# Attention with interleaved MLP work: which max product of a half cycle without filling goes to the filling's PSUM bank

## The chip, the cores and the metric

The kernel runs on one core of a Trainium2 chip. The metric is the device time of one execution in microseconds (us), lower is better. The engines are PE (TensorE: matmul, with its weight loads, PEld, beside it), DVE (VectorE), ACT (ScalarE), POOL (GpSimd) and SP (SyncE, which issues transfers here). PE writes its products to PSUM, which has eight banks of 128 x 512 float32 numbers; DVE and ACT read them there. A bank can take a new product only when the last reader of the old one is done, so a product often waits for a reader.

## The reference

One transformer block with adaptive layer norm, in float32, on 2048 rows of width 512. Attention has 32 query heads of width 16 and a single shared key and value head; the MLP has 1376 hidden units.

```python
def _A_ref(x, wq, wk, wv, wo):              # 32 heads, Dh = 16, one key and value head
    q = (x @ wq).reshape(B, S, H, Dh).transpose(0, 2, 1, 3)
    k = x @ wk
    v = x @ wv
    scores = jnp.einsum("bhqd,bkd->bhqk", q, k) * (Dh ** -0.5)
    p = softmax(scores, axis=-1)
    o = jnp.einsum("bhqk,bkd->bhqd", p, v)
    return o.transpose(0, 2, 1, 3).reshape(B, S, H * Dh) @ wo

def _B_ref(x, w1, b1, w2, b2):
    return gelu(x @ w1 + b1) @ w2 + b2

sa, ca, ga, sb, cb, gb = silu(c) @ w_mod    # six rows of 512
x = x + ga * _A_ref(layernorm(x) * (1 + ca) + sa, wq, wk, wv, wo)
x = x + gb * _B_ref(layernorm(x) * (1 + cb) + sb, w1, b1, w2, b2)
```

## The kernel before

The queries are cut into 8 blocks of 256 rows, and each block into 8 units of 4 heads: 64 units. The softmax takes each row's true maximum, so all scores are computed twice, once for the maximum and once for the exponential:

- **Max products** (`m`, line 509): a 128 x 512 piece of scores, rows of queries against 512 keys. A DVE reduction (`mx`, line 514) takes the maximum of each row. The maxima go through a transpose and POOL into rows of the query tile `qst`, so that the second score product subtracts them by itself. Max products run several units ahead of their exponentials.
- **Score products** (`e`, line 589): keys against queries. ACT takes the exponential (`p`, line 590).
- **Value products** (`acc`, line 601): eight for each pair of key tiles, from `p` and the values.

Both kinds of score product use 64 of PE's 128 rows; side 0 and side 1 (the last number of an `m` or `e` name) run beside each other.

All engines run in the order in which the Python code records the instructions. A loop over units and pairs of key tiles writes one **cycle** per turn, as two **half cycles**. Each half cycle holds four `e` products, as a rule four `m` products and, after them, the eight `acc` products of the pair before (each two weight loads and products in the trace). In the trace a half cycle can be taken from its first `e` product to that of the next one.

Between these the kernel records **filling**: the rest of the work of a block whose attention is done (output projection `wops`, second layer norm and its transposes `tp`, the MLP's products `w1ps` and `w2ps`), and query projections `qps` early on. A job hands its products over in batches of about six (or four transposes); a batch is spread over the two half cycles of a cycle, half of the rows in each. Where no job has a batch ready, which a job says by asking for some turns of delay, both half cycles are written by the function `plain`. `clock` counts turns, four to a cycle. `queue` lists the jobs, each with the turn at which it goes on and a mark for a delay of two turns or more ("planned"); `holder` holds a job that must not be interrupted.

PSUM's banks are given out by tags: three banks for `m` in rotation, three for `e` (`e0` to `e2`) in an order that `plain` passes in `banks`, one (`v`) for `acc`, and one, `x`, for the filling. In `plain`, `maxes(s, n)` makes a list of n max products of side s, and `issue` merges the two lists. In a half cycle with two max products on each side the order of PE's queue is: e, e, m (side s, the first of `ms`), m (side t, the first), e, m (side t, the last), m (side s, the last), e. Sides are s = 1 and t = 0. Line 1332 may send the last max product of side t, the third of the four, to bank x. It does so where no job is held and where no planned job is due within two turns (`soon`).

Of the kernel before, what the change touches and what calls it, by code (L numbers as in the profile page):

```python
# [48 lines left out]
def adaln_mqa_mlp(  # L49
# [16 lines left out]
    _, S, D = x.shape  # L66
# [71 lines left out]
    clock = [0]  # L138
# [10 lines left out]
    def due():  # L149
        now = [p for p in pending if p[0] <= clock[0]]  # L150
        pending[:] = [p for p in pending if p[0] > clock[0]]
        for _, fn in now:
            fn()
# [26 lines left out]
    def half(one, s):  # L180

        ps, a, b_, first_, last_ = one
        rows = slice(64 * s, 64 * s + 64)
        nc.tensor.matmul(ps, a[rows], b_[rows], start=first_ and s == 0, stop=last_ and s == 1)  # L184
# [391 lines left out]
    def sexp(u, K, j, s, bank):  # L576

        w = blocks[units[u][0]][1]
        qst = qsts[u]
        assert u in placed  # L580
        if (u, K) not in ptiles:
            ptiles[u, K] = att.tile([P, 2, 2, 512], F32, name=f"p{u}_{K}", tag="p", bufs=3)
        e = psum.tile([P, 512], F32, name=f"e{u}_{K}_{j}_{s}", tag="x" if bank == "x" else f"e{bank}", bufs=1)
        rows = slice(64 * s, 64 * s + 64)
        if w == 512:
            kt, rhs = K, qst[rows, j, :]
        else:
            kt, rhs = 2 * K + j, qst[rows].rearrange("p j n -> p (j n)")
        nc.tensor.matmul(e, ks[rows, kt * P:(kt + 1) * P], rhs, start=True, stop=True)  # L589
        nc.scalar.activation(ptiles[u, K][:, j, s, :], e, AF.Exp, scale=0.25)  # L590
# [488 lines left out]
    def prep_w2():  # L1079
        rp = wts_pool["rest"]  # L1080
        wfs = {}

        def load(f):
            fw = min(P, F - f * P)
            wf = wfs[f] = rp.tile([P, D], F32, name=f"w2f{f}", tag="wf", bufs=3)
            if fw < P:
                nc.gpsimd.memset(wf, 0.0)
            nc.sync.dma_start(out=wf[:fw], in_=w2[f * P:f * P + fw, :])

        def work(f):  # L1090
            nc.gpsimd.tensor_tensor(out=wfs[f], in0=wfs[f], in1=gb, op=ALU.mult)
            split(w2H[:, f, :], w2L[:, f, :], wfs[f], nc.gpsimd, nc.gpsimd)

        return prepare(NF, load, work)
# [3 lines left out]
    queue = []  # L1098
    holder = []
# [14 lines left out]
    def resume():  # L1114

        go_on(holder[0])

    def advance():

        for job in holder or list(queue):  # L1120
            while not held and job[0] <= clock[0] and go_on(job):
                pass
            if held or holder:
                break
# [4 lines left out]
    def take():  # L1129
        advance()  # L1130
        return held.pop() if held else None
# [3 lines left out]
    mp = Max()  # L1135
# [129 lines left out]
    def products(batch):  # L1265

        return sum(b_.shape[-1] * (4 if b_.dtype == F32 else 1) for _, _, b_, _, _ in batch) / 512
# [7 lines left out]
    def issue(*groups):  # L1275

        at = [0.0] * len(groups)
        groups = [list(g) for g in groups]
        while any(groups):
            g = min((g for g in range(len(groups)) if groups[g]), key=lambda g: at[g])  # L1280
            length, fn = groups[g].pop(0)
            fn()
            at[g] += length

    def mixture(a, b):

        out = []
        while a or b:
            if a:
                out.append(a.pop(0))  # L1290
            if b:
                out.append(b.pop(0))
        return out

    def end_step(u, K):

        pv(u, K)
        if K == steps[u] - 1:
            finish_unit(u)
            if units[u][1] == NQ - 1:  # L1300
                put_off(rest(units[u][0], units[u][0] == len(blocks) - 1))

    behind = None
    for u in range(NU):
        for K in range(0, steps[u], 2):
            goal = lead[u] + (lead[u + 1] - lead[u]) * (K + 2) / steps[u]
            goal = min(goal, first[u + QBUFS] if u + QBUFS < NU else first[NU])
            n = max(0, 2 * round((goal - mp.done) / 2))

            def maxes(s, n, first_=1.0, held=None):  # L1310
                return [(1.0 if i else first_, lambda i=i: mp.step(s, held if i == 2 else None)) if mp.has(s) else (0.0, lambda: None)
                        for i in range(n)]

            def exps(s, which):
                return [(1.0, lambda K=K, j=j, bank=bank: sexp(u, K, j, s, bank)) for K, j, bank in which]

            def halves(batch, s):

                total = products(batch)
                ahead = AHEAD if total > BATCH - 0.5 else (BATCH - (1.5 if batch[-1][4] else 0.5)) / total  # L1320
                return [(ahead * products([one]), lambda one=one: half(one, s)) for one in batch]

            def plain(s, K, t, n, banks):

                a, b_, c_, d = banks
                one = mixture(exps(s, [(K, 0, a), (K, 1, c_)]), maxes(s, n))
                other = maxes(t, n)

                soon = any(planned and time <= clock[0] + 2 for time, _, planned in queue)
                if not holder and not soon and mp.has(t) and n > 1:  # L1330
                    other[-1] = 1.0, lambda: mp.step(t, tag="x", bufs=1)
                issue(one, exps(t, [(K, 0, b_)]) + other + exps(t, [(K, 1, d)]))

            X, Y = K, K + 1

            due()
            batch = take() if behind else None
            if batch:  # L1340
                groups = [mixture(maxes(1, n // 2, 0.0), exps(1, [(X, 0, 0), (X, 1, 1), (Y, 0, 2)])),
                          halves(batch, 0) + exps(0, [(X, 0, 0)])]
                issue(*(reversed(groups) if batch[0][3] else groups))
            else:
                plain(1, X, 0, (n + 2) // 4, (1, 2, 0, 1))
            clock[0] += 1
            due()
            if behind:
                end_step(*behind)
            clock[0] += 1  # L1350
            due()
            if batch:

                reduces = [] if batch[-1][4] else None

                def go_on_():
                    resume()
                    for fn in reduces or ():
                        fn()

                issue(mixture(maxes(0, n // 2, 0.0, reduces), exps(0, [(X, 1, 0), (Y, 0, 1), (Y, 1, 2)])),
                      halves(batch, 1) + [(0.0, go_on_)] + exps(1, [(Y, 1, 0)]))
                advance()
            else:
                plain(1, Y, 0, n // 4, (2, 0, 1, 2))
            clock[0] += 1
            due()
            end_step(u, X)
            behind = (u, Y)
            clock[0] += 1  # L1370
            if state["mods"] and state["q"] == 0 and w2H is None:
                w2H = att.tile([P, NF, D], F32R, name="w2H", tag="bigH")
                w2L = att.tile([P, NF, D], F32R, name="w2L", tag="bigL")
                preps["w2"] = prep_w2()
            if clock[0] >= prepared[0] + PREP and weights and weights[0] in preps:
                prepared[0] = clock[0]
                if next(preps[weights[0]], 0) == 0:
                    weights.pop(0)
# [51 lines left out]
```

## Time and profile before

| what | value |
|---|---|
| time, median of 3 runs | 1599.63 us (1597.88 to 1600.57) |
| the profiled execution's own time | 1599.49 us |
| span of the profiled execution | 1597.6 us |
| busy: PE, DVE, ACT, POOL | 1560.3, 1412.9, 1203.0, 666.1 us |
| granted TensorE clock, mean | 0.996 |
| max products, and their reductions on DVE | 2048 each, 682 ns a reduction |
| exponentials on ACT | 2048, 599 ns each |
| first half cycles without filling in a block, ahead of `tp` | at 324.48 and 327.78 us (block 0) |
| those ahead of `w1ps` | at 342.11 and 345.06 us (block 0) |

A row of the page's list of groups reads: line, engine, operation, tile written <- tiles read, shapes, count | busy us, mean ns of one | idle time of the engine just before these instructions, and what ended it. A row of the timeline reads: start in us, length in us, engine, line, operation, tiles, how many are merged in the row, and in brackets the idle time ahead of it with what ended that. PE's ends are modelled. A row of a windows answer reads: stretch in us, its length, then for PE, PEld, DVE, ACT and POOL the busy time with the number of instructions, then the granted clock and the transfers.

### The profile page before, as it was taken

To read this page: it belongs to the slowest core of one execution; us is meant where nothing else is said; L and a number is where in the kernel's file an instruction comes from. 1 tells how busy PE (TensorE), PEld (TensorE's weight loads), DVE (VectorE), ACT (ScalarE), POOL (GpSimd) and SP (SyncE) were. 2 spreads that over 40 slices of the span, in tenths; PEclk is the share of its full clock that TensorE was granted. 3 is DMA by queue.
4 is the path that set the end of the run, shared out by engine and by line. 5 is a ranking of instruction groups with operands and counts; after the bars stand their busy time and mean duration, and the time that the engine had idled before them with its cause. 6 is when DMAs were issued, how large, how long until landed. Compare 5 with 4: busy or idle time off the path is not lost.

```text
span 1597.6 us, 41064 instructions
## 1 busy us (share of the span) xinstructions
PE 1560.3 (98%) x16369; PEld 1006.3 (63%) x16369; DVE 1412.9 (88%) x2473; ACT 1203.0 (75%) x2393; POOL 666.1 (42%) x1176
## 2 busy tenths in 40 slices
PE   5999999999999999999999999999999999999998
PEld 3466665557665676657665676656666576656667
DVE  6899999899999998999989999999999999999715
ACT  5577778778777887778877887778877787778853
POOL 4445344747422571246413462234602474225711
PEclk8999999999999999999999999999999999999999
DMA  7136312313022220303112120213112130122232
GB/s 257 73 109 205 117 68 71 125 32 107 17 63 65 68 68 25 103 17 106 32 44 84 53 85 22 78 42 98 42 35 91 42 98 18 62 72 64 80 132 74
DMA packets 79285, 121.59 MB, mean 76 GB/s; under 512 B 15774, under 2 KB 52382, under 8 KB 78836
## 3 DMA queue, kind: packets, MB, share of 16 engines
q1 hardware_dynamic: 79076, 118.95, 23.2%
q8 instruction: 128, 2.10, 0.6%
q14 instruction: 65, 0.53, 0.1%
q10 hardware_dynamic: 16, 0.00, 0.0%
HBM read 91.13 MB, written 27.27 MB: 74 GB/s over the span
## 4 chain that ended last, share of the span: by engine, by line
PE 90%; DVE 6%; DMA 2%; POOL 1%; SPq 1%; ACT 0%; issue 0%; DVEq 0%; POOLq 0%
PE acc L601 30%; PE m L509 22%; PE e L589 17%; PE w1ps L184 8%; DVE mx L514 5%; PE w2ps L184 4%; PE wops L184 2%; PE qps L184 1%; PE w2ps L178 1%; DMA xt<-in_A_x_dram 1%; PE w1ps L178 1%; PE tp L184 1%; PE kps L160 1%; DMA qst<-dq 1%; DVE st L807 0%; DMA os<-drs 0%
## 5 line engine op out<-in xcount | busy, mean ns | idle before, releaser
L514 DVE TENSOR_REDUCE mx<-m 128x1 f32<-128x512 f32 x2048 | 1271.4, 682 | 107.6 <-PE m L509 81.3
L590 ACT ACTIVATE p<-e 128x512 f32<-128x512 f32 x2048 | 1069.4, 599 | 311.1 <-PE e L589 233.2
L509 PE MATMUL m<-ks,qst 64*128 64x512 f32 x2048 | 823.9, 425 | 17.4 <-DVE mx L514 11.0
L589 PE MATMUL e<-qst,ks 64*128 64x512 f32 x2048 | 739.1, 409 | 2.8 <-ACT p L590 1.5
L601 PE MATMUL acc<-p,va 128*32 128x256 f32 x8192 | 550.5, 386 | 0.6 <-DMA qst<-dq 0.6
L509 PEld LDWEIGHTS m<-ks,qst 64*128 64x128 f32 x2048 | 364.1, 184 | 185.8 <-DVE mx L514 157.0
L589 PEld LDWEIGHTS e<-qst,ks 64*128 64x128 f32 x2048 | 366.6, 185 | 85.2 <-ACT p L590 59.5
L601 PEld LDWEIGHTS acc<-p,va 128*32 128x32 f32 x8192 | 214.9, 109 | 220.6 <-issue 115.7
L184 PE MATMUL w1ps<-h2H,w1t 64*128 64x256 f32 x1232 | 236.3, 288 | 0.0
L558 POOL TENSOR_SCALAR mt<-turned 8x32 f32<-8x32 f32 x256 | 53.2, 208 | 362.4 <-DVE turned L564 350.4
L184 PEld LDWEIGHTS w1ps<-h2H,w1t 64*128 64x128 f32 x1232 | 184.2, 185 | 31.7 <-issue 23.0
L184 PE MATMUL w1ps<-h2L,w1t 64*128 64x256 f32 x616 | 169.4, 275 | 0.0
L184 PE MATMUL w2ps<-w2H,gH 64*128 64x512 f32 x286 | 118.1, 413 | 0.0
L184 PE MATMUL w2ps<-w2L,gH 64*128 64x512 f32 x286 | 117.4, 411 | 0.0
L184 PE MATMUL w2ps<-w2H,gL 64*128 64x512 f32 x286 | 117.4, 410 | 0.0
L184 PEld LDWEIGHTS w1ps<-h2L,w1t 64*128 64x128 f32 x616 | 113.8, 185 | 0.0
L920 POOL TENSOR_SCALAR tt<-tt 128x256 f32<-128x256 f32 x77 | 31.1, 404 | 162.8 <-ACT tt L919 162.8
L744 POOL TENSOR_TENSOR os<-os 128x256 f32<-128x256 f32 x28 | 20.6, 734 | 100.9 <-DMA os<-drs 100.2
L921 POOL TENSOR_TENSOR tt<-tt,z 128x256 f32<-128x256 f32 x77 | 57.1, 741 | 6.4
L135 POOL TENSOR_TENSOR gL<-z,gH 128x256 fp32r<-128x256 f32 x77 | 56.8, 738 | 6.4
L931 POOL TENSOR_TENSOR z<-tt,z 128x256 f32<-128x256 f32 x77 | 56.5, 733 | 6.0
L930 POOL TENSOR_TENSOR tt<-tt,z 128x256 f32<-128x256 f32 x77 | 56.7, 736 | 0.0
(188 smaller groups left out, 1498.2 us busy)
## 6 DMA issues: line engine op xcount, KB each, us to landing
w1t<-dw SPq DMA_DIRECT2D x82, 512.0 KB
qst<-dq SPq DMA_DIRECT2D x128, 64.0 KB
do<-oc SPq DMA_DIRECT2D x64, 128.0 KB
dw<-w1s SPq DMA_DIRECT2D x11, 512.0 KB
xt<-in_A_x_dram SPq DMA_DIRECT2D x4, 1024.0 KB
dq<-qH SPq DMA_DIRECT2D x16, 256.0 KB
dq<-qL SPq DMA_DIRECT2D x16, 256.0 KB
qst<-dq SPq DMA_DIRECT2D x128, 32.0 KB
```

The lines of the kernel that those rows point to most:

```text
L135: eng_l.tensor_tensor(out=dst_l, in0=src, in1=raw(dst_h), op=ALU.subtract)
L178: nc.tensor.matmul(ps, a, b_, start=first_, stop=last_)
L184: nc.tensor.matmul(ps, a[rows], b_[rows], start=first_ and s == 0, stop=last_ and s == 1)
L509: nc.tensor.matmul(m, qsts[u][rows, j, t * P:(t + 1) * P], ks[rows, kc * 512:(kc + 1) * 512], start=True, stop=True)
L514: nc.vector.tensor_reduce(out=self.mx[u][:, i, kc:kc + 1], in_=m, axis=AX.X, op=ALU.max)
L558: nc.gpsimd.tensor_scalar(out=mt[:, g:g + 32], in0=turned[g:g + 4 * T, :], scalar1=1.0, scalar2=0.0, op0=ALU.mult, op1=ALU.add)
L589: nc.tensor.matmul(e, ks[rows, kt * P:(kt + 1) * P], rhs, start=True, stop=True)
L590: nc.scalar.activation(ptiles[u, K][:, j, s, :], e, AF.Exp, scale=0.25)
L601: ins = nc.tensor.matmul(accs[u][32 * cidx:32 * cidx + 32, :], va[:, kt, :], rhs, start=kt == 0, stop=kt == NKT - 1)
L921: nc.gpsimd.tensor_tensor(out=tt, in0=tt, in1=z, op=ALU.mult)
L930: nc.gpsimd.tensor_tensor(out=tt, in0=tt, in1=z, op=ALU.mult)
L931: nc.gpsimd.tensor_tensor(out=z, in0=tt, in1=z, op=ALU.add)
```

## The change

In `plain`, the max product that goes to bank x is now the first of side s instead of the last of side t. In PE's queue this is the first of the four in place of the third. The condition on planned jobs falls away, so bank x is also used in the last half cycles ahead of new filling. The first product of the filling then finds a max product in bank x, where it found the filling's own last tile before.

```diff
             def plain(s, K, t, n, banks):
 
                 a, b_, c_, d = banks
-                one = mixture(exps(s, [(K, 0, a), (K, 1, c_)]), maxes(s, n))
-                other = maxes(t, n)
-
-                soon = any(planned and time <= clock[0] + 2 for time, _, planned in queue)
-                if not holder and not soon and mp.has(t) and n > 1:
-                    other[-1] = 1.0, lambda: mp.step(t, tag="x", bufs=1)
+                ms, other = maxes(s, n), maxes(t, n)
+
+                if not holder and mp.has(s) and n > 1:
+                    ms[0] = 1.0, lambda: mp.step(s, tag="x", bufs=1)
+                one = mixture(exps(s, [(K, 0, a), (K, 1, c_)]), ms)
                 issue(one, exps(t, [(K, 0, b_)]) + other + exps(t, [(K, 1, d)]))
```

Every engine keeps its instructions and their order; what changes is the bank of a product and so what it waits for. 34 of the 2048 max products went to bank x before, 62 do now. The 28 new ones are one in each of four half cycles in each of the seven blocks 0 to 6: two ahead of the filling that begins with `tp`, two ahead of that which begins with `w1ps`. In these half cycles the four max products had three banks, and the fourth took the bank of the first of the same half cycle. Now each of the four takes the bank of the product at its own place in the half cycle before it. For block 0:

| max product (start) | takes the bank of, before | takes the bank of, now |
|---|---|---|
| first of the half cycle at 324.48 | first of the half cycle before | first of the half cycle before (bank x) |
| second | second of the half cycle before | second of the half cycle before |
| third | fourth of the half cycle before | third of the half cycle before |
| fourth | first of the same half cycle | fourth of the half cycle before |
| first of the half cycle at 327.78 | second of the half cycle before | first of the half cycle before (bank x) |
| fourth | first of the same half cycle | fourth of the half cycle before |
| first of the half cycle at 342.11 | second of the half cycle before | last tile `tp` of the filling, read by ACT (line 867) |
| fourth | first of the same half cycle | fourth of the half cycle before |

In PE's rows this shows where the engine that is waited for changes. The first place is the end of the half cycle at 327.78, where the filling of block 0 goes on with its first transpose (`tp`; the name in brackets is the engine whose progress the row waits for, `DMAHW` is a transfer):

```order
 L601 MATMUL acc_4504<-p_6_4692,va 32x256 [waits DMAHW2_49]
 L601 MATMUL acc_4504<-p_6_4692,va 32x256 x3
-L184 MATMUL tp_0_0_0_4762<-ident,xh_0_0_4237 128x128 [waits Pool_49]
+L184 MATMUL tp_0_0_0_4762<-ident,xh_0_0_4237 128x128 [waits DVE_49,Pool_49]
 L509 MATMUL m_1_1_0_1_4764<-ks,qst_158 128x512 [waits DVE_49]
 L589 MATMUL e_0_0_1_4768<-qst_161,ks 128x512 [waits Activation_49]
```

The transpose still waits for POOL, which makes its input, and now for DVE too, since the reduction of a max product has to leave bank x. The second place is the half cycle at 342.11, right behind the transposes:

```order
 L589 MATMUL e_4_0_1_4948<-qst_161,ks 128x512 [waits Activation_49]
 L589 MATMUL e_4_0_0_4951<-qst_161,ks 128x512 [waits Activation_49]
-L509 MATMUL m_0_1_0_1_4954<-ks,qst_159 128x512 [waits DVE_49]
+L509 MATMUL m_0_1_0_1_4954<-ks,qst_159 128x512 [waits PE_49,Activation_49]
 L509 MATMUL m_0_1_0_0_4957<-ks,qst_159 128x512 [waits DVE_49]
 L589 MATMUL e_4_1_1_4960<-qst_161,ks 128x512 [waits Activation_49]
```

Here the first max product waits for ACT, which reads the last `tp` tile out of bank x, instead of for a reduction.

## The prediction

> **What bounds the kernel now.** I read the page first, for the engines and their costliest groups:
>
> ```profile
> PE 1560.3 (98%) x16369; PEld 1006.3 (63%) x16369; DVE 1412.9 (88%) x2473; ACT 1203.0 (75%) x2393; POOL 666.1 (42%) x1176
> L514 DVE TENSOR_REDUCE mx<-m 128x1 f32<-128x512 f32 x2048 | 1271.4, 682 | 107.6 <-PE m L509 81.3
> L509 PEld LDWEIGHTS m<-ks,qst 64*128 64x128 f32 x2048 | 364.1, 184 | 185.8 <-DVE mx L514 157.0
> ```
>
> PE looks full at 98%, but the weight loads of the max products sat idle for 157.0 us until a reduction on DVE gave a bank back. Such a wait is paid only where PE has nothing else queued, so the next view is the timeline of PE and ACT, first in a half cycle without filling that does use bank x:
>
> ```profile
> 319.26 0.50 PE L589 MATMUL e<-qst,ks 64*128 64x512 f32 x2
> 320.45 0.49 PE L589 MATMUL e<-qst,ks 64*128 64x512 f32 x1
> 320.87 1.07 PE L601 MATMUL acc<-p,va 128*32 128x256 f32 x16
> 321.87 0.51 PE L589 MATMUL e<-qst,ks 64*128 64x512 f32 x2
> 319.80 2.06 ACT L590 ACTIVATE p<-e 128x512 f32<-128x512 f32 x4 [0.54 <-PE e L589]
> 246.10:287.88 41.78, 41.64 (x389) 21.10 (x385) 40.46 (x71) 33.79 (x66) 18.94 (x29) 1.00 0.30 89
> ```
>
> It lasts 321.87 - 319.26 = 2.61 us. The fourth e product starts 1.19 us in, because there are three e banks and it takes the first product's, which its exponential (319.80 to about 320.4) holds; from there the acc products run, 1.42 us to the next half cycle. The last row is a windows answer over 16 such half cycles (time, then busy time of PE, PEld, DVE, ACT and POOL): 41.78 / 16 = 2.61. So **2.61 us is the floor**, set by the loop e product, exponential, e product. Max products and DVE fit inside it.
>
> Now two half cycles without filling that do not use x, the ones ahead of the transposes (`tp`):
>
> ```profile
> 324.48 0.54 PE L589 MATMUL e<-qst,ks 64*128 64x512 f32 x2
> 325.75 1.09 PE L509 MATMUL m<-ks,qst 64*128 64x512 f32 x2 [0.32 <-DVE mx L514]
> 326.35 0.50 PE L589 MATMUL e<-qst,ks 64*128 64x512 f32 x1
> 327.78 0.50 PE L589 MATMUL e<-qst,ks 64*128 64x512 f32 x2
> 329.29 0.50 PE L509 MATMUL m<-ks,qst 64*128 64x512 f32 x1 [0.55 <-DVE mx L514]
> 330.71 0.37 PE L184 MATMUL tp<-ident,xh 64*128 64x128 f32 x1
> 325.01 1.57 ACT L590 ACTIVATE p<-e 128x512 f32<-128x512 f32 x3 [0.54 <-PE e L589]
> 323.24 4.84 DVE L514 TENSOR_REDUCE mx<-m 128x1 f32<-128x512 f32 x8
> 328.54 2.48 DVE L514 TENSOR_REDUCE mx<-m 128x1 f32<-128x512 f32 x4 [0.46 <-PE m L509]
> ```
>
> They last 327.78 - 324.48 = 3.30 and 330.71 - 327.78 = 2.93 us. With three m banks for four max products, the fourth needs the bank of the *first of its own half cycle*: product, reduction, product. Reductions follow each other every (4.84 - 0.68) / 7 = 0.594 us. The first product's is the fifth of the eight, so it ends at 323.24 + 4 x 0.594 + 0.68 = 326.30, and the fourth product and the e product queued behind it start at 326.35. Afterwards DVE itself idles (0.46 us before 328.54): DVE is not the limit, the number of banks is.
>
> The same happens in the two half cycles ahead of `w1ps`. Windows answers, laid from the first e product to the filling's first product, cover the seven blocks (first, last and sum of each set of seven):
>
> ```profile
> 324.48:330.71 6.23, 5.27 (x52) 2.41 (x48) 5.77 (x11) 4.31 (x8) 6.13 (x4) 1.00 0.06 18
> ...
> 1425.39:1431.65 6.26, 5.29 (x53) 2.41 (x49) 5.79 (x11) 4.31 (x8) 6.17 (x5) 1.00 0.13 32
> sum 43.66, PE 37.02 PEld 16.91 DVE 40.44 ACT 30.22 POOL 43.11; mean PE 5.29 PEld 2.42 DVE 5.78 ACT 4.32 POOL 6.16
> 342.11:347.99 5.88, 5.07 (x52) 2.20 (x48) 4.90 (x9) 4.97 (x10) 2.24 (x4) 1.00 0.10 26
> ...
> 1443.03:1448.91 5.88, 5.06 (x52) 2.20 (x49) 5.05 (x10) 4.98 (x10) 2.24 (x4) 1.00 0.03 8
> sum 41.17, PE 35.42 PEld 15.38 DVE 34.45 ACT 34.84 POOL 15.67; mean PE 5.06 PEld 2.20 DVE 4.92 ACT 4.98 POOL 2.24
> ```
>
> That is 43.66 + 41.17 = 84.83 us in 28 half cycles, 3.03 each, and block 0 stands for all seven. The granted clock is 1.00 throughout.
>
> **The change part by part.** No instruction is added or removed, on any engine. Three things happen to banks.
>
> *(a) The 28 half cycles get a fourth bank.* Each max product then waits for the reduction of the product at its own place one half cycle earlier. In the stretch at 324.48 the fourth product needs the fourth of the eight reductions, which ends at 323.24 + 3 x 0.594 + 0.68 = 325.70, so it starts at 325.75. The fourth e product needs the first exponential (325.01 + 0.60), which is earlier. So it starts at 325.75 instead of 326.35, and with the 327.78 - 326.35 = 1.43 us behind it the next half cycle starts at 327.18: **0.60 gained**. In that one the last reduction of before ends at 323.24 + 7 x 0.594 + 0.68 = 328.08, 0.29 us before the fourth products are due at 327.18 + 1.19 = 328.37; so it runs at the floor and `tp` starts at 327.18 + 2.61 = 329.79, **0.92 us earlier in all**. What is late next is the exponential.
>
> Ahead of `w1ps` ACT is behind, because the modulation of the filling (L867) went first:
>
> ```profile
> 342.12 0.49 PE L589 MATMUL e<-qst,ks 64*128 64x512 f32 x2
> 342.45 0.39 PE L509 MATMUL m<-ks,qst 64*128 64x512 f32 x2
> 343.05 0.50 PE L589 MATMUL e<-qst,ks 64*128 64x512 f32 x1 [0.21 <-ACT p L590]
> 343.63 0.50 PE L589 MATMUL e<-qst,ks 64*128 64x512 f32 x1
> 345.06 0.51 PE L589 MATMUL e<-qst,ks 64*128 64x512 f32 x2
> 346.56 0.50 PE L509 MATMUL m<-ks,qst 64*128 64x512 f32 x1 [0.53 <-DVE mx L514]
> 347.99 0.38 PE L184 MATMUL w1ps<-h2H,w1t 64*128 64x256 f32 x1
> 341.48 1.03 ACT L867 ACTIVATE h<-tp,sb,cb 128x256 f32<-128x256 f32 x2
> 342.38 2.57 ACT L590 ACTIVATE p<-e 128x512 f32<-128x512 f32 x5
> 342.88 2.48 DVE L514 TENSOR_REDUCE mx<-m 128x1 f32<-128x512 f32 x4 [0.53 <-PE m L509]
> ```
>
> The second exponential of the five, the one that frees the fourth e product's bank, ends at about 342.38 + 0.49 + 0.62 = 343.49, so that product starts at 343.54 at best instead of 343.63: only **0.09 gained**, since a wait for ACT stands right behind the one removed. The next half cycle (345.06 to 347.99, 2.93) drops to 2.61: **0.32 gained**. Per block 0.92 + 0.41 = 1.33 us, and 7 x 1.33 = **9.3 us**.
>
> *(b) Bank x passes to the first max product, at new waits.* In the stretch at 342.12 that product takes x from `tp`, which the two L867 activations read until 341.48 + 1.03 = 342.51. It starts at about 342.57 instead of 342.45. Behind it in PE's queue stand a max product and the third e product, and that one cannot start before 343.05 anyway (ACT): the delay is hidden, with 0.48 us to spare; uncovered it would cost 0.12 x 7 = 0.8 us. `tp` and `w1ps` find x last used by a max product instead of one long read. Its reduction is the first in the half cycle ahead, about 328.00 to 328.68 against `tp` at 329.79: 1.1 us to spare. I take nothing for (b).
>
> *(c) In the half cycles that used x before*, only the place of x moves. All four banks still come round once per half cycle, so the floor of 2.61 stays: nothing. One wait goes: the first filling of all takes x right behind them.
>
> ```profile
> 291.74 2.38 POOL L135 TENSOR_TENSOR onL<-os,onH 128x1024 fp32r<-128x1024 f32 x1
> 293.45 0.47 PE L184 MATMUL wops<-woH,onH 64*128 64x512 f32 x1 [0.28 <-DVE mx L514]
> 294.17 0.49 PE L184 MATMUL wops<-woH,onL 64*128 64x512 f32 x1
> ```
>
> The 0.28 us before 293.45 goes, but the second wops product needs POOL's onL, which ends at 294.12. Whatever is saved ahead of it is waited for there. I take nothing; it happens once.
>
> The profiled execution took 1599.49 us (span 1597.6 and 1.9 around it), 0.14 below the median of the runs shown. 1599.5 - 9.3 = **1590.2 us**. Bounds: all 28 half cycles at the floor would be 84.83 - 28 x 2.61 = 11.8, so 1587.7; the other end is the first rival's.
>
> **A rule weighed.** The Trainium skill, page "VectorE: DVE Perf Modes", section "The DRAIN you can't avoid", says that a Vector operation does not begin until the pipe of the one before is empty, and makes an exception for one that is not held. The trace sides with the exception: 0.594 us from start to start where one lasts 0.682. By the bare rule the time would be the first rival's.
>
> **The rivals.**
> *DVE becomes the bound.* If four reductions took their full duration in turn, 4 x 0.682 = 2.73 us would replace the floor of 2.61. A block's four would take 2.73 x 3 + 2.85 = 11.04 instead of 84.83 / 7 = 12.12, a gain of 7 x 1.08 = 7.6: 1591.9 us. For: DVE is busy for 5.77 of 6.23 us there. Against: four follow in 2.48 us, and DVE idles ahead of them.
>
> *The gain is waited away behind.* As at 294.17, what follows may not be ready sooner. `tp` needs POOL's normalised rows:
>
> ```profile
> 324.57 4.15 POOL L819 TENSOR_SCALAR xh<-x,mv,rs 128x512 f32<-128x512 f32 x2
> ```
>
> They end at 328.72, so `tp` at 329.79 has 1.07 us to spare. Were that gone, the first 0.92 would be lost in each block and 7 x 0.41 = 2.9 remain: 1596.6; with only the second lost, 1599.5 - 7 x 0.92 = 1593.1; with both, 1599.5. The filling behind them keeps its instructions and its order, and moves up as it is.
>
> *The filling stalls on x.* If DVE lagged at the half cycle's end by more than the 1.1 us of (b), `tp` and `w1ps` would wait at the head of PE's queue, and everything behind them one for one. Beyond 1.1 + 0.66 = 1.8 us of lag the 14 entries would eat the gain of 9.3; at 2.1 they cost 14 x 1.0 and the kernel is 4.7 us slower, 1604. For: statistics on DVE go in between in the half cycles before. Against: DVE idles 0.46 us one half cycle later, and the product in x is now the first to be reduced.
>
> **How the numbers follow.** Forecast, waits go as in (a): 0.70. DVE bound: 0.13. Waited away: 0.12. Stall on x: 0.05. About 0.2%, 3.2 us, can be told from no change, so the first two are faster (0.83), the third the same (0.12), the last slower (0.05). The range runs from the bound of 1587.7 to 1593.1, the end with the second gain lost, which takes in the DVE rival; the three runs shown lie up to 1.8 us from their median, so I widen it by 1.3 on each side, to 1586.5 and 1594.5. That leaves out 0.17.
>
> **What would show it.** The half cycles now 3.30, 2.93, 2.94 and 2.93 us should last 2.70, 2.61, 2.85 and 2.61; in the timeline the wait ahead of the fourth products should be for ACT, not DVE (but for the first of the four); `tp` and `w1ps` should show no wait for mx, and filling should keep its pace. A first half cycle that stays above 3 us, or a `tp` that waits for POOL or DVE, would prove me wrong.

## The result and the profile after

| | before | changed |
|---|---|---|
| time, median | 1599.73 us (1597.88 to 1603.47) | 1589.37 us (1588.75 to 1590.04) |
| the profiled execution's own time (span) | 1599.49 (1597.6) | 1590.01 (1588.0) |

The ratio is 0.9934, with a 95% interval of 0.9921 to 0.9947: faster by 8.5 to 12.6 us (six runs of each kernel). The forecast was 1590.2, in a range of 1586.5 to 1594.5.

The page of the changed kernel, its line of busy times and the group of the max products' weight loads:

```profile
PE 1564.1 (98%) x16369; PEld 1010.2 (64%) x16369; DVE 1409.8 (89%) x2473; ACT 1201.1 (76%) x2393; POOL 666.2 (42%) x1176
L509 PEld LDWEIGHTS m<-ks,qst 64*128 64x128 f32 x2048 | 362.2, 184 | 171.2 <-DVE mx L514 139.6
```

PE's share is 98% as before, which tells nothing; the idle time that a reduction ended fell from 157.0 to 139.6 us. Where it fell is seen in the timelines of PE, ACT, DVE and POOL, in the two half cycles ahead of `tp` of block 0 (start, length, engine, line, operation):

```profile
324.69 0.54 PE L589 MATMUL e<-qst,ks 64*128 64x512 f32 x2
325.36 1.09 PE L509 MATMUL m<-ks,qst 64*128 64x512 f32 x2
325.96 0.50 PE L589 MATMUL e<-qst,ks 64*128 64x512 f32 x1
327.39 0.50 PE L589 MATMUL e<-qst,ks 64*128 64x512 f32 x2
328.57 0.49 PE L589 MATMUL e<-qst,ks 64*128 64x512 f32 x1
330.00 0.37 PE L184 MATMUL tp<-ident,xh 64*128 64x128 f32 x1
327.92 2.06 ACT L590 ACTIVATE p<-e 128x512 f32<-128x512 f32 x4 [0.63 <-PE e L589]
324.03 6.66 DVE L514 TENSOR_REDUCE mx<-m 128x1 f32<-128x512 f32 x11
324.79 4.15 POOL L819 TENSOR_SCALAR xh<-x,mv,rs 128x512 f32<-128x512 f32 x2
```

The first lasts 2.70 us instead of 3.30, the second 2.61 instead of 2.93. In the first the fourth max product, with the fourth `e` product behind it at 325.96, still waits for a reduction, but for an older one, the third of the eleven in the row (324.03 + 2 x 0.598 + 0.68 = 325.91, where 0.598 is (6.66 - 0.68) / 10). In the second the idle 0.55 us ahead of the fourth max product is gone, and the fourth `e` product starts 1.18 us in, 0.05 behind the first exponential (327.92 + 0.60): the exponential is the next wait, as in the half cycle at 319.26, which had four banks before (1.19 us in). DVE now runs eleven reductions without a gap.

The two half cycles ahead of `w1ps`, timeline of PE and ACT:

```profile
341.39 0.50 PE L589 MATMUL e<-qst,ks 64*128 64x512 f32 x2
341.84 0.50 PE L509 MATMUL m<-ks,qst 64*128 64x512 f32 x2
342.33 0.50 PE L589 MATMUL e<-qst,ks 64*128 64x512 f32 x1
342.81 0.49 PE L589 MATMUL e<-qst,ks 64*128 64x512 f32 x1
344.24 0.51 PE L589 MATMUL e<-qst,ks 64*128 64x512 f32 x2
346.84 0.38 PE L184 MATMUL w1ps<-h2H,w1t 64*128 64x256 f32 x1
340.75 1.03 ACT L867 ACTIVATE h<-tp,sb,cb 128x256 f32<-128x256 f32 x2
341.65 2.57 ACT L590 ACTIVATE p<-e 128x512 f32<-128x512 f32 x5
```

They last 2.85 and 2.60 us. The first max product comes 0.45 us into its half cycle, where it came 0.33 in: it waits for the two activations of L867 to leave bank x (340.75 + 1.03 = 341.78). The third `e` product behind it starts 0.94 us in, as before.

The windows of all seven blocks, first and last of each set and its sum (columns as above):

```profile
324.69:330.00 5.31, 5.20 (x53) 2.60 (x49) 5.31 (x10) 4.13 (x8) 5.21 (x3) 1.00 0.09 27
...
1417.28:1422.59 5.31, 5.21 (x54) 2.60 (x50) 5.31 (x10) 4.13 (x8) 5.23 (x4) 1.00 0.10 31
sum 37.17, PE 36.46 PEld 18.17 DVE 37.17 ACT 28.91 POOL 36.59; mean PE 5.21 PEld 2.60 DVE 5.31 ACT 4.13 POOL 5.23
341.39:346.84 5.45, 5.45 (x53) 2.55 (x49) 4.55 (x9) 4.89 (x10) 2.25 (x4) 1.00 0.07 23
...
1433.96:1439.42 5.46, 5.46 (x52) 2.54 (x48) 4.71 (x10) 4.90 (x10) 2.25 (x4) 1.00 0.03 8
sum 38.15, PE 38.15 PEld 17.77 DVE 32.06 ACT 34.28 POOL 15.70; mean PE 5.45 PEld 2.54 DVE 4.58 ACT 4.90 POOL 2.24
```

37.17 + 38.15 = 75.32 us for the 28 half cycles, where they took 84.83: 9.5 us, against 9.6 us between the two spans (1597.6 and 1588.0). All else takes 1512.7 us in one trace and 1512.8 in the other (1588.0 - 75.3, and 1597.6 - 84.8). That the two agree so closely is chance: in the traces below the same rest lies between 1511.2 and 1514.6 us. The medians lie 10.4 us apart, 0.9 more than the half cycles account for; the runs of the changed kernel spread over 1.3 us and those of the kernel before over 5.6, so this difference is within their scatter.

### The profile page after: what moved, and what is told of

It reads as the page before. It is cut to its first block, busy times and chain, and to the rows that moved or that the text cites. A ratio compares the mean times of both kernels' runs of the same rounds, so it can differ in the third digit from the quotient of the medians.

```text
span 1588.0 us, 41078 instructions
## 1 busy us (share of the span) xinstructions
PE 1564.1 (98%) x16369; PEld 1010.2 (64%) x16369; DVE 1409.8 (89%) x2473; ACT 1201.1 (76%) x2393; POOL 666.2 (42%) x1176
## 4 chain that ended last, share of the span: by engine, by line
PE 91%; DVE 5%; DMA 2%; POOL 1%; SPq 1%; ACT 0%; issue 0%; DVEq 0%; POOLq 0%
PE acc L601 30%; PE m L509 22%; PE e L589 18%; PE w1ps L184 8%; PE w2ps L184 4%; DVE mx L514 4%; PE wops L184 2%; PE qps L184 2%; PE w2ps L178 1%; PE tp L184 1%; PE w1ps L178 1%; DMA xt<-in_A_x_dram 1%; PE kps L160 1%; DMA qst<-dq 0%; DVE st L807 0%; PE wops L178 0%
## 5 line engine op out<-in xcount | busy, mean ns | idle before, releaser
L509 PEld LDWEIGHTS m<-ks,qst 64*128 64x128 f32 x2048 | 362.2, 184 | 171.2 <-DVE mx L514 139.6
```

Source lines behind the costliest of these rows:

```text
L509: nc.tensor.matmul(m, qsts[u][rows, j, t * P:(t + 1) * P], ks[rows, kc * 512:(kc + 1) * 512], start=True, stop=True)
```

## The experiments

Each run was compared with the kernel before on the same chip, whose median there was 1599.65 us for the kernels from "x at the third place" to "x at the fourth place", 1599.35 for the next and 1600.22 for the last. The table sets them beside each other; the half cycles are differences of start times in the timelines, means of the seven blocks, in the order of a block (two ahead of `tp`, two ahead of `w1ps`). "Rest" is the span of the profiled execution without the 28 half cycles.

| kernel | half cycles, us | 28 of them | rest of the span | median time | ratio to before (interval) |
|---|---|---|---|---|---|
| before | 3.29, 2.95, 2.95, 2.94 | 84.9 | 1512.7 | 1599.73 | |
| changed | 2.69, 2.62, 2.85, 2.60 | 75.3 | 1512.7 | 1589.37 | 0.9934 (0.9921 to 0.9947) |
| x at the third place | 2.70, 2.85, 2.86, 2.80 | 78.5 | 1511.6 | 1592.69 | 0.9953 (0.9941 to 0.9965) |
| place alone | 3.30, 2.95, 2.95, 2.94 | 85.0 | 1511.3 | 1599.60 | 0.9999 (0.9990 to 1.0008) |
| ahead of `tp` alone | 2.71, 2.62, 2.94, 2.94 | 78.5 | 1511.2 | 1592.15 | 0.9954 (0.9941 to 0.9966) |
| x at the fourth place | 2.70, 3.45, 2.86, 3.39 | 86.8 | 1514.6 | 1600.82 | 1.0004 (0.9994 to 1.0014) |
| changed, and modulation off ACT | 2.69, 2.62, 2.61, 2.61 | 73.7 | 1511.8 | 1587.31 | 0.9923 (0.9910 to 0.9937) |
| before, and modulation off ACT | 3.29, 2.95, 2.95, 2.94 | 85.0 | 1512.0 | 1599.32 | 0.9999 (0.9990 to 1.0008) |

The changed kernel itself ran once more beside the kernel "changed, and modulation off ACT", as a yardstick:

> The changed kernel itself, for a comparison on the same chip with the run beside it: 1589.4 us, 9 to 11 us below the kernel before. Theory and rivals expect the same.

It gave 1589.28 us (1588.17 to 1589.85), ratio 0.9934 (0.9922 to 0.9947).

In the code below, `...` marks what is left out, and `name=...` and the like shorten a line.

### Half the change: the condition, and the place

The first kernel drops the condition on planned jobs but leaves bank x with the third max product. Against the kernel before:

```diff
-                soon = any(planned and time <= clock[0] + 2 for time, _, planned in queue)
-                if not holder and not soon and mp.has(t) and n > 1:
+                if not holder and mp.has(t) and n > 1:
                     other[-1] = 1.0, lambda: mp.step(t, tag="x", bufs=1)
```

> The condition on planned jobs falls away as in the change, but bank x stays with the third max product of the half cycle. Theory (fourth bank gives the time, its place decides what the filling's first product waits for): the four half cycles of a block run as in the change, but tp waits for the third reduction, which in the changed kernel ends 2.70 us after the start of the half cycle at 327.39, against 2.61 when tp is due, and w1ps for one that ends at 2.65: about 0.15 and 0.10 us lost, 7 x 0.25 = 1.7 us, so a gain of 9.3 - 1.7 = 7.6 us, near 1592. Rival (only the number of banks counts): as the change, near 1589.5 to 1590. Rival (the place alone counts): no gain, 1599.7.

1592.69 us. The first half cycles of each pair run as in the changed kernel. The second ones, whose end is the filling's first product, take 2.85 and 2.80 instead of 2.62 and 2.60: 7 x (0.23 + 0.20) = 3.0 us, where 1.7 was expected. The direction and the two places are those of the theory; the size is off, for a reason that the kernel with x at the fourth place shows.

The second kernel moves the place and keeps the condition. Against the changed kernel, as in the next three edits:

```diff
-                if not holder and mp.has(s) and n > 1:
+                soon = any(planned and time <= clock[0] + 2 for time, _, planned in queue)
+                if not holder and not soon and mp.has(s) and n > 1:
```

> Bank x goes to the first max product, but only where it was used before (no planned job due within two turns). Theory: no change, 1599.7 within 0.5 us; the 28 half cycles keep 3.30, 2.93, 2.94 and 2.93 us; only the wait of the first wops product in block 0 goes, 0.3 us, and is waited for again at POOL's onL. Rival (the place alone counts): a gain of several us.

1599.60 us, and the means of the 28 half cycles stay within 0.01 us. The place gains nothing by itself (interval of the ratio 0.9990 to 1.0008). The one wait that it removes, ahead of the first filling of block 0, is lost behind it as forecast; timeline of PE and POOL:

```profile
292.30 0.49 PE L184 MATMUL wops<-woH,onH 64*128 64x512 f32 x1
293.20 0.50 PE L184 MATMUL wops<-woH,onL 64*128 64x512 f32 x1 [0.17 <-POOL onL L135]
290.78 2.38 POOL L135 TENSOR_TENSOR onL<-os,onH 128x1024 fp32r<-128x1024 f32 x1
```

The first `wops` product no longer waits for DVE, and the second one stands until 0.04 us after POOL's onL (290.78 + 2.38 = 293.16).

### One pair of half cycles alone

The job says which filling comes next, and bank x is withheld ahead of `w1ps`.

```diff
+                state["w1 next"] = False
                 yield 8
...
+                state["w1 next"] = True
                 yield 4
...
-                if not holder and mp.has(s) and n > 1:
+                soon = any(planned and time <= clock[0] + 2 for time, _, planned in queue)
+                if not holder and not (soon and state.get("w1 next")) and mp.has(s) and n > 1:
```

> The change, but without bank x in the two half cycles ahead of w1ps; those ahead of tp have it. Theory: the parts add up. The half cycles ahead of tp last 2.70 and 2.61, those ahead of w1ps 2.94 and 2.93 as before: gain 7 x 0.92 = 6.4 us, near 1593.2. Rival (what is gained ahead of tp is waited away behind it): under 3 us.

1592.15 us, 7.5 below the kernel before. The pair ahead of `tp` falls as in the changed kernel, the other stays, and the 28 take 84.9 - 78.5 = 6.4 us less, the number expected. Nothing of it is waited away behind `tp`.

### The price of the place

Bank x goes to the last max product of side s, the fourth of the half cycle.

```diff
-                    ms[0] = 1.0, lambda: mp.step(s, tag="x", bufs=1)
+                    ms[-1] = 1.0, lambda: mp.step(s, tag="x", bufs=1)
```

> The change, but bank x goes to the fourth max product in place of the first; same number of products in x. Theory: tp and w1ps now wait at the head of PE's queue for the fourth reduction, which in the changed kernel ends 3.30 and 3.25 us after the start of the half cycle ahead, against 2.60 when they are due: 0.74 and 0.69 us lost, 7 x 1.43 = 10.0 us, which eats the gain of 9.3: near 1600, between 1599 and 1601.5. Rival (only the number of banks counts): as the change, near 1589.5 to 1590.

1600.82 us. With as many max products in x as the change has, the whole gain is gone. Its timeline ahead of `tp` in block 1, and the waits of PE over the whole span (engine, line, what it waited for: total us, times, longest):

```profile
514.10 1.06 PE L601 MATMUL acc<-p,va 128*32 128x256 f32 x14
515.93 0.34 PE L184 MATMUL tp<-ident,xh 64*128 64x128 f32 x1 [0.77 <-DVE mx L514]
511.51 4.27 DVE L514 TENSOR_REDUCE mx<-m 128x1 f32<-128x512 f32 x7
```

```profile
PE w1ps L184 <- DVE mx L514: 5.0, 7, 0.7
PE tp L184 <- DVE mx L514: 4.6, 6, 0.8
PE tp L184 <- POOL x L823: 0.8, 1, 0.8
```

`tp` stands at the head of PE's queue until the last reduction has left x. One of the seven waits of `tp` is put down to POOL's line 823, which does not make the transposes' input; there too `tp` starts 0.15 us after a reduction. Against the kernel before, the first half cycle of each pair gains (0.59 and 0.09) and the second loses (0.50 and 0.45). The rest of the span is about 2 us longer than in the other traces. The excess lies ahead of the first filling product of all (`qps`), which starts at 87.44 us, where the kernel before has it at 85.07. Of these 2.4 us, 0.89 are the same stall: `qps` too waits here for a reduction to leave x (rows below). The remainder is not explained.

The seventh reduction ends at 511.51 + 4.27 = 515.78, and `tp` starts 0.15 us later. The expectation had reckoned 0.05, the distance of before (326.30 to 326.35). With x at the third and at the fourth place `tp` and `w1ps` have two engines to wait for, and the wait for DVE is an instruction of its own ahead of the product. The same trace shows it (lengths in ns, on the queue of PE's weight loads), with the weight load behind it, and a product that waits for x and for DVE alone, the first `qps`:

```profile
L184 PEldq EVENT_SEMAPHORE  x1: 51/51/51, 515.8 to 515.8; - x1
515.89 0.18 PEld L184 LDWEIGHTS tp<-ident,xh 64*128 64x128 f32 x1 [1.22 <-POOL x L823]
84.31 3.07 DVE L514 TENSOR_REDUCE mx<-m 128x1 f32<-128x512 f32 x5
87.44 0.50 PE L184 MATMUL qps<-h0H,wqH 64*128 64x512 f32 x1 [0.89 <-DVE mx L514]
```

`qps` starts 0.06 us after its reduction (84.31 + 3.07 = 87.38), with no such instruction ahead. At all 14 places of `tp` and `w1ps` the weight load comes 0.11 to 0.12 us after the reduction and the product 0.03 us later. So two waits cost about 0.09 us more than one; 14 x 0.09 = 1.3 us, which is what the third place lost beyond its expectation (3.0 - 1.7 = 1.3). The wait instruction accounts for 0.05 us of it; what makes up the rest is open.

### What is late next

The third half cycle of a block stops at 2.85, for which the prediction blamed L867 on ACT. The edit gives the second half of the modulation to a DVE copy and POOL, as the first half has it.

```diff
-                if not fast and dp == 0:
+                if not fast:
                     src = rp.tile([P, 2, HQ], F32, name=..., tag="ot", bufs=2)
                     nc.vector.tensor_copy(out=src, in_=ps)
...
-                    if fast or dp:
+                    if fast:
                         nc.scalar.activation(h32, ps[:, d2, :], AF.Identity, scale=..., bias=...)
```

> The changed kernel, with the second half of the filling's modulation taken from ACT: a DVE copy out of bank x and two POOL operations, as the first half has it, in place of two activations from x (L867). Theory (ACT's two activations hold up the exponentials in the third of the four half cycles, 2.85 instead of 2.61): that half cycle falls to 2.61, 7 x 0.24 = 1.7 us less than the change, near 1587.8; POOL needs about 1.1 us more for its rows, which end about 344.8 against w1ps at 346.6. Rival (2.85 is not ACT's doing): as the change, 1589.4. Rival (the added DVE copy of 0.69 us or POOL's 1.1 us come late): slower than the change.

1587.31 us, beside 1589.28 for the changed kernel. The intervals of the two ratios overlap (0.9910 to 0.9937 and 0.9922 to 0.9947), so the gain rests on the traces: 73.7 us for the 28 half cycles, where the changed kernel has 75.3. Timeline of PE, ACT, DVE and POOL in the same half cycle:

```profile
340.28 0.49 PE L589 MATMUL e<-qst,ks 64*128 64x512 f32 x2
341.46 0.50 PE L589 MATMUL e<-qst,ks 64*128 64x512 f32 x1
342.88 0.50 PE L589 MATMUL e<-qst,ks 64*128 64x512 f32 x2
345.49 0.38 PE L184 MATMUL w1ps<-h2H,w1t 64*128 64x256 f32 x1
340.81 2.06 ACT L590 ACTIVATE p<-e 128x512 f32<-128x512 f32 x4 [0.55 <-PE e L589]
339.24 0.68 DVE L862 COPY tc<-tp 128x512 f32<-128x512 f32 x1
343.14 0.73 POOL L135 TENSOR_TENSOR h2L<-h,h2H 128x256 fp32r<-128x256 f32 x1
```

ACT waits for PE again and the half cycle lasts 2.60 (2.61 in the mean): the floor. POOL's last operation ends at 343.87, 1.6 us before `w1ps`. By its median this is the fastest of the kernels, 12 us below the one before.

The same edit without the change tells whether ACT alone held that half cycle up. The two ran side by side:

> The kernel before, with only the modulation's second half taken from ACT as in the run that combined it with the change. Theory (two waits stand behind each other in the third of the four half cycles: first for a reduction of the same half cycle, then, 0.09 us earlier, for ACT): taking the ACT wait away alone gains nothing; the four half cycles keep 3.29, 2.95, 2.94 and 2.94 us within 0.03, and the time is that of the kernel before, 1599.6, within 1 us. Rival (ACT alone holds that half cycle up): 2.61 there and 7 x 0.33 = 2.3 us gained, 1597.3.

> The change together with the modulation off ACT, again, beside the run without the change: 1587.3 us, 12 us below the kernel before; third half cycle 2.61.

1599.32 us without the change (ratio in the table), and the third half cycle keeps 2.95; 1587.85 with it, ratio 0.9922 (0.9909 to 0.9934), and 2.61 there. Two waits stood one behind the other: taking ACT's away gains nothing while the reduction's is there, taking the reduction's away gains 0.09 us while ACT's is there, and both together gain 0.33.

## Why the prediction was right, point by point

**The bound.** The fourth bank was worth the time: the place alone gave 0.9999, the bank ahead of `tp` alone 6.4 us of the trace. The place decides whether the gain is kept: with as many max products in x, the fourth place gave 1.0004. The Trainium skill, page "Perfetto Trace Analysis", section "Optimization Strategy", says that a gap which repeats on the engine that should be full can be a sign of too little PSUM. The gap of 0.55 us ahead of the fourth product was one, and it went.

**Part (a), the sum.** The four half cycles were forecast at 2.70, 2.61, 2.85 and 2.61 and came at 2.69, 2.62, 2.85 and 2.60. The forecast of 9.3 us compares with 9.5 in the trace. The small remainder is in the windows of before: 12.12 us a block in the mean, where block 0, on which the steps were worked, has 12.11, and in sums rounded to 0.01.

**Part (b), the new waits.** They cost nothing, with the spare time that was worked out. The reduction that frees x for `tp` is the eighth of the eleven in the row: 324.03 + 7 x 0.598 + 0.68 = 328.9, 1.1 us before `tp` at 330.00. The delay of the first max product by L867 stayed covered by the third `e` product. PE's waits over the whole span of the changed kernel name no `tp` of line 184 and no `w1ps`, as forecast. The step would have failed with another place for x: the third costs 3.0 us, the fourth all of the gain.

**Part (c).** Right: nothing, and the 0.3 us at the first `wops` is paid to POOL.

**DVE as the bound.** This rival was wrong in its price and partly right in kind. DVE is busy for all of 37.17 us in the windows ahead of `tp`, working off a lag: the row of block 0 has eleven reductions, where two half cycles bring eight. In the first half cycle PE still waits for that lag, 2.69 us instead of 2.61, as part (a) had it. The second runs at the floor, because reductions follow each other every 0.598 us, four in 2.39. The Trainium skill, page "VectorE: DVE Perf Modes", section "The DRAIN you can't avoid", lets an operation that is not held start before the pipe of the one before is empty; the trace agrees, with 0.598 us from start to start of operations that last 0.68. By the page's bare rule four would take the rival's 2.73, an estimate.

**Waited away behind.** It did not happen at `tp` or `w1ps`: POOL's rows ended at 324.79 + 4.15 = 328.94, 1.06 us early, as forecast. It is seen once, at the first `wops` of block 0, where it takes up differences of the start as well.

**The stall on x.** The mechanism is real and its point was placed rightly: the prediction had the gain eaten when the reduction that frees x comes 1.8 us later, and the fourth product's comes 3 x 0.598 = 1.8 us after the first's; with x at the fourth place the gain is gone. What brought it about is the place of the product in the half cycle, not a lag of DVE.

## What to carry to other kernels

When a stage has one buffer fewer than products in a round, the last product waits for the first of its own round; look for this where a loop that normally has the buffer is denied it, and work the gain out against the next wait in line, not against the wait's own length. When a buffer is lent to a loop just before its owner returns, lend it to the product that is consumed first. Two waits that end within 0.09 us of each other hide a third of a microsecond between them: when one is removed and little is gained, the other is worth trying.

## What the runs showed of the hardware that was not expected

A filling's first product that waits for two engines began 0.15 us after the end of the reduction that freed its bank (515.78 to 515.93), where products with one wait began 0.05 and 0.06 us after it (326.30 to 326.35, and 87.38 to 87.44). A wait instruction of 0.05 us stands ahead of the first. DVE was busy without a gap for 6.66 us while the half cycle at 327.39 kept to 2.61 us, which the exponentials on ACT set.
